# Attention and two feed-forward stages on one core: moving the first h products, the last output tiles and a score wait

## The chip, the cores and the metric

The kernel runs on one core of a Trainium2 chip. The metric is the time of one execution in device microseconds (us). The kernel before takes 922.23 us, the median of three runs from 921.72 to 922.34.

Engines are named as in the profile: PE is TensorE's matmul, PEld its weight load, DVE VectorE, ACT ScalarE, POOL GpSimd, SP SyncE, which issues the DMAs. A name such as SPq is the sequencer of that engine.

## The reference

Batch 4, 8 heads, 576 positions, head dimension 64; then 2304 tokens of width 512.

```python
scores = scale * np.matmul(q, k.transpose(0, 1, 3, 2))
cum = np.cumsum(np.maximum(s, 0.0), axis=-1)
bias = -(cum[:, :, :, None] - cum[:, :, None, :])
scores = np.where(causal, -1000000000.0, scores + np.minimum(bias, 0.0))
attn = softmax(scores)                     # max taken off, sum + 1e-9
x = (attn @ v), heads side by side         # (2304, 512)
x = ((x @ w1) * (x @ w2)) @ w3 @ w_out     # inner width 1024
h = x @ w_in                               # width 2048
out = (h - np.tanh(h)) @ w_out2            # (2304, 512)
```

## The kernel before

All instructions are collected as operations with the buffers they read and write, a priority (a small number goes first), and for some a choice of engines (ACT, DVE or POOL). A list planner (class Plan) plays them through with costs and the numbers in PARAM, picks on each engine the ready operation with the smallest priority, and writes the result out. The order on each engine, and which engine does an operation, is fixed from then on. On the chip an engine works its list in order and waits where data are late. Where the planner expects PE to wait in the first 66 us, it puts dummy matmuls (`filler`, line 576) into the list.

Stages, in order of time:

1. Attention, head by head (`head`), 32 heads. For the eight heads of batch 0 (`full`) a score tile is one matmul in full f32 over 69 rows (line 688; line 686 for the first head): 64 rows of q and k, and five rows of bias. The five bias rows of k are written by two small DMAs (query tiles 0 to 2, and 3 to 4), the five rows of q hold a pattern that picks one of them for each query tile. In the other batches the operands are split into two parts of f32r (`split`: a high part by `copy`, a low part by `sub`, lines 410 to 414) and there are two matmuls (lines 690, 691). Transposes are line 745, the products with v line 772.
2. `products` (line 826): x @ w1 and x @ w2 with split operands, three matmuls for each product. The weights w1, w2 are converted from 64-bit inputs on ACT and DVE first (`convert`, lines 515 to 522). The result goes to DRAM (c_d).
3. w3 @ w_out in one matrix (lines 941 to 943), and operands for stage 5.
4. `x2_block(j)`, j = 0 to 5, 384 tokens each (lines 978 to 980): c @ (w3 @ w_out), two halves n of four groups d of twelve matmuls. Priority 1.2e6 + 100 j + 10 n + d. The results are copied to xs (j = 0, 1) or to xd tiles, which are stored to DRAM (xf_d).
5. Three passes of eight steps (`step`, 24 in all). h = x @ w_in goes by Strassen-like seven products of half size (`product`, line 1055, six matmuls each), with operands x2b (seven tiles) and ws (13 slots, seven used by a step; loaded from ws_d in the order ORDER). Products are accumulated on PSUM banks a, b, c; `taken` copies a bank to a temporary (on ACT mostly), `plus` (line 1064, DVE) adds a bank and a temporary. Each of the four sums of a step goes through `gated` (lines 1078 to 1087: u, sq, th, pg, mk on ACT and DVE, then gh and gl), and then three output tiles of three matmuls each (lines 1095 to 1097, with voh and vol, the split w_out2) are accumulated on banks 0 to 5. After a pass the six banks are copied to osb tiles (two of them) and stored.

SBUF is handed out by pools that open and close in the course of the kernel. `pre` (left) opens before the x2 products and holds seven x2b tiles, ws0 to ws6, and the first NPRE = 12 of 16 w_out2 pairs. `p2` (right) opens when the x2 products have let go of their operands (xp, wap and cp closed) and holds all else of stage 5: the other ws slots, gh, gl, u, sq, th, pg, mk, osb. The seven temporaries (cst0 to 2, asb0 to 3) live from stage 2 to the end.

The parts around the change:

Of the kernel before, what the change touches and what calls it, by code (L numbers as in the profile page):

```python
# [40 lines left out]
PARAM = dict(tail=346719, dsub2=2687.6, dcopy2=-363.2, dother2=15239, act2=-1777.4, pool2=4728.0, cs=1176.5, xs=-29.3, layw=10048, x2p=785.3, nwst=3, late=778.7,  # L41
             gate=4314.0, cst=6240.0, ramp0=1010.9, ramp1=-512.9, dsub=4382.6, dsub0=-2390.3, dcopy=-1480.1, dcopy0=-572.5, dother=1106.1, dother0=-2029.8,
             spi=2833.6, lay=0, layp=641747, layf=473733, dve0=1000.0, early=120052, raw0=0, rawp=-700.0, ng=8, nosb=2, cut=(), convq=2713.8, natb=8, nfull=8,
             wap=1402502, dve=1000.0, act=-598.5, pool=-114.4, sem=160.0, pesem=180.0, slow=1.1, convp=3444.2, npre=12, nbias=3, keep=0.5, ff=0.0, fu=66000,
             wlast=0, kbp=-210.2, qk=2491.2, kb=-1761.7, rv=-1179.0, st=83.8, fl=756.2, iv=1391.7, pv=-1105.8, ml=4388.9, bw=370.0, ntr=3, actb=1, actn=0,
             spp=3043.5, ne=2, nsb=2, ncf=5, outlag=187.2, o_qk=-577.9, o_kb=647.6, o_rv=179.7, o_iv=-2316.9, o_fl=-889.6, o_pv=-374.3, o_ml=-281.5, o_st=829.5,
             o_c0=-132.5, o_c1=211.6, o_c2=404.2, o_c3=3145.8, o_c4=-302.4, o_c5=1092.9, o_c6=-321.1, o_c7=-538.4, o_c8=-309.2, o_c9=568.4, o_c10=-644.8,
             o_c11=721.4, o_c12=620.5, o_c13=-386.2, o_c14=-1078.1, o_c15=-517.3, o_h0=-2746.5, o_h1=-2197.2, o_h2=507.3, o_h3=211.0, o_h4=-153.0, o_h5=1351.8,
             o_h6=-1038.9, o_h7=-501.6, o_h8=-600.0, o_h9=726.1, o_h10=-463.4, o_h11=308.3, o_h12=1634.4, o_h13=837.2, o_h14=-1715.4, o_h15=-171.3, o_h16=-831.4,
             o_h17=198.0, o_h18=-178.6, o_h19=1097.2, o_h20=517.6, o_h21=-1252.5, o_h22=177.5, o_h23=337.0, o_h24=-1368.9, o_h25=-531.3, o_h26=724.9, o_h27=-159.5,  # L50
             o_h28=2096.8, o_h29=-111.9, o_h30=-510.2, o_h31=-973.2)
# [289 lines left out]
def tile_kernel(ctx, tc, qk, v, s, w1, w2, w3t, w_out, w_in, w_out2, out):  # L341
# [108 lines left out]
    cst_r = abp.ring("cst", 3, [P, TB])  # L450
    asb_r = abp.ring("asb", 4, [P, TB])
# [4 lines left out]
    rqk = [att.buf(f"rqk{i}", [P, 2 * S], n=3) for i in range(2)]  # L456
# [29 lines left out]
    xs_r = cp.ring("xs", 10, [P, XB])  # L486
    xd_r = cp.ring("xd", 4, [P, XB])
# [3 lines left out]
    p2 = Pool("p2", "right")  # L491
    x2b = [p_.buf(f"x2b{i}", [P, 2, 2, XB], F32R, n=4) for i, p_ in enumerate([pre] * 7 + [p2])]
# [14 lines left out]
    osb_r = p2.ring("osb", PARAM["nosb"], [P, DM], n=2)  # L507
# [90 lines left out]
    for e in e2[:1] + [None] + e2[1:]:  # L598
        if e is None:
            zero([lambda: ssum.t], [20], [ssum], -5, 1.0)  # L600
            for R in rqk:
                a = 0 if R is rqk[0] else S
                pl.op([("POOL", 1040.0 if a == 0 else 560.0, lambda R=R, a=a: nc.gpsimd.memset(R.t[D:D + 5, a:], 0.0))], w=[(R, (1, 2))], prio=-2300)
        else:
            zero([later(e, EOFF[0], EOFF[0] + D, low)], [D], [(e, 0)], -10 if e is e2[0] else 92, r=scan)
# [32 lines left out]
    def role(n, b):  # L638
        return PARAM[n] + (PARAM["o_" + n] if b == 0 else 0.0)

    def head(h, full, groups=(0, 1)):
# [32 lines left out]
        def softmax_tile(t):  # L674
            q0, q1 = QT[t]
            nq = q1 - q0
            p_ = pr + role("st", b) * t
            bi, bo = msk, (512 if nq < P else S) - q1
            pieces = [(0, q1)] if q1 <= 512 else [(0, HALF), (HALF, S)]
            for n, (k0, k1) in enumerate(pieces):  # L680
                bk = s_ring.next()

                def mm(bk=bk, k0=k0, k1=k1):
                    o_ = bk.t[:nq, :k1 - k0]
                    if one:
                        nc.tensor.matmul(bk.t[:, :k1 - k0], rq()[:D + 5, q0:q0 + P], rk()[:D + 5, k0:k1], start=True, stop=False)
                    elif full:
                        nc.tensor.matmul(bk.t[:, :k1 - k0], rq()[:D + 5, q0:q0 + P], rk()[:D + 5, k0:k1], start=True, stop=True)  # L688
                    else:
                        nc.tensor.matmul(o_, Q.t[:, q0:q1], KH.t[:, k0:k1], start=True, stop=False)  # L690
                        nc.tensor.matmul(o_, Q2.t[:NR, q0:q1], KL.t[:NR, k0:k1], start=False, stop=True)  # L691
                if one:
# [3 lines left out]
                    pe(f_mm4(k1 - k0), mm, [R], [bk], p_ - 2000.0)  # L696
# [261 lines left out]
    x2_ring = Ring(bank[0:8])  # L958
    held = {}

    def x2_block(j):
# [21 lines left out]
        for d in range(KC):  # L983
            x = (xd_r if p else xs_r).next()
            held[l, d] = x
            copy(lambda x=x, d=d: x.t, lambda d=d: bks[d].t[:, :XB], XB, [bks[d]], [x], 1.9e5, psum=True)
            if p:
                dma(lambda d=d: xf_d.t[p, l, d], lambda x=x: x.t, P * XB * 4, [x], [(xf_d, (p * 2 + l) * KC + d)], 2.2e5, row=1536, issue=580.0)
        if j == 1:
            for kg in range(2):  # L990
                operands(kg, [held[y, z * 2 + kg] for z, y in ((0, 0), (0, 1), (1, 0), (1, 1))], xs_r, 2.2e5,
                         lambda i, x, kg=kg: split(lambda: X0[i].t[:, kg, 0], (X0[i], kg * 2), lambda: X0[i].t[:, kg, 1], (X0[i], kg * 2 + 1), lambda: x.t, XB, [x], 2.2e5, kind="xs"))
# [55 lines left out]
    def step(p, fp, pos, X, W):  # L1048
        pr, last = 3.0e5 + pos, p == NPAIR - 1 and fp == NFP - 1

        def product(n, i, bk, first):
# [4 lines left out]
            pe(f_op(6 * f_mm(XB)), mm, [W[i], X[i]], [bk], 2.0e6 + pos + n // 2 * 45 + n % 2)  # L1056
# [64 lines left out]
        if fp == NFP - 1:  # L1121
            for l in range(2):
                for n in range(3):
                    ob, t0, bk = osb_r.next(), p * 2 * XB + l * XB + n * P, bank[l * 3 + n]
                    for a, z in ((0, 256), (256, 512)) if last else ((0, 512),):
                        copy(lambda ob=ob, bk=bk, a=a, z=z: ob.t[:, a:z], lambda bk=bk, a=a, z=z: bk.t[:, a:z], z - a, [bk], [(ob, int(a > 0))] if last else [ob], pr, psum=True)
                    dma(lambda t0=t0: out[t0:t0 + P, :], lambda ob=ob: ob.t, P * DM * 4, [ob], [], 0)

    for p in range(NPAIR):
# [7 lines left out]
        for fp in range(NFP):  # L1137
# [3 lines left out]
            W = {}  # L1141
            for n, i in enumerate(ORDER):
# [49 lines left out]
```

## Time and profile before

| | us |
|---|---|
| median of three runs | 922.23 |
| the profiled execution | 921.88 |
| its span, first to last instruction | 920.2 |
| PE busy | 906.6 (99%) |
| PEld busy | 790.6 (86%) |
| DVE busy | 790.7 (86%) |
| ACT busy | 549.0 (60%) |
| POOL busy | 112.1 (12%) |
| mean granted clock of PE | 0.997 |

Busy is the time in which an engine had an instruction in hand. Matmuls overlap, and their ends are modelled: a matmul of 384 columns is shown as 0.33 us, while the next starts 0.17 us later. The distance of starts tells PE's pace better than the busy time.

### The profile page before, as it was taken

The numbers are of one execution on the slowest core, as the hardware profiler recorded it, in microseconds if no ns is written. First come the engines' busy times: TensorE is split into PE (matmuls) and PEld (weight loads), VectorE is DVE, ScalarE is ACT, GpSimd is POOL, SyncE is SP. The second block draws the span as 40 slices with busy tenths as digits, with TensorE's granted clock in tenths as the row PEclk, the third lists the DMA queues.
The fourth block names the chain that finished last, engine by engine and source line by source line (L and its number), as shares of the span: only waits on it lengthen the run. The fifth ranks groups of instructions, "written<-read, shape, count | busy, mean of one in ns | idle before, by whom it ended". The sixth has DMA issues, their size and how long they took to land.

```text
span 920.2 us, 15850 instructions
## 1 busy us (share of the span) xinstructions
PE 906.6 (99%) x5174; PEld 790.6 (86%) x5174; DVE 790.7 (86%) x1884; ACT 549.0 (60%) x1292; POOL 112.1 (12%) x106
## 2 busy tenths in 40 slices
PE   9999999999999999999999989999999999999996
PEld 7777788888887888988999988989898998989885
DVE  8999999899999599989536999999998878787874
ACT  6998854343423013555446577777787667776765
POOL 1000044545442172000000000000000000000000
PEclk9999999999999999999999999999999999999998
DMA  7677766456565458898877595787977448644401
GB/s 222 202 227 194 217 203 213 130 186 212 177 220 161 154 179 279 275 296 282 270 231 236 189 306 173 255 275 236 387 236 260 116 117 304 200 116 123 115 12 69
DMA packets 102948, 189.94 MB, mean 206 GB/s; under 512 B 10594, under 2 KB 50690, under 8 KB 102867
## 3 DMA queue, kind: packets, MB, share of 16 engines
q1 hardware_dynamic: 102866, 188.94, 64.8%
q8 instruction: 41, 0.67, 0.3%
q14 instruction: 41, 0.33, 0.1%
HBM read 137.20 MB, written 48.01 MB: 201 GB/s over the span
## 4 chain that ended last, share of the span: by engine, by line
PE 89%; DVE 5%; DMA 3%; ACT 1%; issue 1%; SPq 0%; ACTq 0%; DVEq 0%
PE bank L826 21%; PE bank L1055 18%; PE bank L1096 7%; PE bank L1097 7%; PE bank L1095 7%; PE bank L745 5%; PE bank L772 5%; PE bank L979 2%; PE bank L978 2%; PE bank L980 2%; PE bank L690 2%; PE bank L688 2%; PE bank L691 2%; PE bank L941 2%; PE bank L942 2%; PE bank L943 2%
## 5 line engine op out<-in xcount | busy, mean ns | idle before, releaser
L1055 PE MATMUL bank<-x2b,ws 128*128 128x384 f32 x1008 | 192.9, 337 | 2.8 <-DMA ws<-ws_d 1.3
L1055 PEld LDWEIGHTS bank<-x2b,ws 128*128 128x128 f32 x1008 | 178.8, 188 | 12.1 <-DVE asb L1064 3.0
L711 ACT ACTIVATE e<-e,nmx 64x64 f32<-64x64 f32 (+4 forms) x160 | 89.1, 558 | 95.6 <-DVE nmx L705 95.0
L1097 PE MATMUL bank<-voh,gl 128*128 128x512 f32 x288 | 113.8, 395 | 0.0
L1096 PE MATMUL bank<-vol,gh 128*128 128x512 f32 x288 | 113.6, 394 | 0.0
L1095 PE MATMUL bank<-voh,gh 128*128 128x512 f32 x288 | 111.9, 389 | 0.0
L410 ACT ACTIVATE gh<-pg 128x384 fp32r<-128x384 f32 x96 | 50.0, 521 | 46.8 <-DVE pg L1087 46.5
L745 PE MATMUL bank<-ident,e 128*128 128x128 f32 (+1 forms) x480 | 75.4, 275 | 0.8 <-ACT e L711 0.7
L705 DVE CUSTOM_DVE_ANT_0 e<-bank,msk 64x64 f32<-64x64 f32 (+4 forms) x160 | 64.7, 420 | 4.5 <-PE bank L691 3.9
L1064 DVE TENSOR_TENSOR asb<-bank,cst 128x384 f32<-128x384 f32 x72 | 40.0, 555 | 33.2 <-PE bank L1055 32.8
L980 PE MATMUL bank<-xh,wal 128*128 128x384 f32 x192 | 64.1, 334 | 0.0
L978 PE MATMUL bank<-xh,wah 128*128 128x384 f32 x192 | 64.1, 334 | 0.0
L979 PE MATMUL bank<-xl,wah 128*128 128x384 f32 x192 | 64.1, 334 | 0.0
L1097 PEld LDWEIGHTS bank<-voh,gl 128*128 128x128 f32 x288 | 54.0, 187 | 11.5
L826 PE MATMUL bank<-xh,w2h 128*128 128x512 f32 (+1 forms) x160 | 63.3, 396 | 0.0
L745 PEld LDWEIGHTS bank<-ident,e 128*128 128x128 f32 (+1 forms) x480 | 53.8, 131 | 11.0 <-ACT e L711 2.3
L826 PE MATMUL bank<-xh,w1h 128*128 128x512 f32 (+1 forms) x160 | 63.1, 394 | 0.1
L1096 PEld LDWEIGHTS bank<-vol,gh 128*128 128x128 f32 x288 | 54.0, 187 | 9.0
L1095 PEld LDWEIGHTS bank<-voh,gh 128*128 128x128 f32 x288 | 54.1, 188 | 8.6
L515 ACT ACTIVATE wt<-wraw 128x512 f32<-128x512 f32 x62 | 41.4, 671 | 31.0 <-DMA wraw<-w3t 16.7
L826 PE MATMUL bank<-xh,w1l 128*128 128x512 f32 (+1 forms) x160 | 59.4, 371 | 0.0
L1087 DVE COPY_PREDICATED pg<-mk,th 128x384 f32<-128x384 uint32 x96 | 57.8, 602 | 1.9
(144 smaller groups left out, 2190.9 us busy)
## 6 DMA issues: line engine op xcount, KB each, us to landing
ws<-ws_d SPq DMA_DIRECT2D x168, 256.0 KB
ws_d<-wst SPq DMA_DIRECT2D x56, 256.0 KB
rqk<-qk SPq DMA_DIRECT2D x24, 576.0 KB
wraw<-w_out SPq DMA_DIRECT2D x24, 512.0 KB
x_d<-x2s SPq DMA_DIRECT2D x28, 384.0 KB
x2b<-x_d SPq DMA_DIRECT2D x14, 768.0 KB
wraw<-w SPq DMA_DIRECT2D x16, 512.0 KB
wraw<-w_in SPq DMA_DIRECT2D x16, 512.0 KB
```

Source lines behind the costliest of these rows:

```text
L705: nc.vector.tensor_tensor_reduce(e.t[:nq, EOFF[t] + k0:EOFF[t] + k1], bk.t[:nq, :k1 - k0], bi.t[:nq, bo + k0:bo + k1], -0.125, 3.0e38 if f ...
L711: act(lambda: nc.scalar.activation(et(), et(), AF.Exp, bias=nmx.t[:nq, i, tm:tm + 1], scale=-1.0, accum_out=ssum.t[:nq, pj, t, i:i + 1]), ...
L745: nc.tensor.transpose(bk.t[:rows, (at + m) * P:(at + m + 1) * P], e.t[:, EOFF[t] + c * P:EOFF[t] + c * P + rows], ident.t)
L826: nc.tensor.matmul(bk.t[:, :w], w_.t[:, k, f * P:(f + 1) * P], x_.t[:, k, :w], start=k == 0 and i == 0, stop=k == KC - 1 and i == 2)
L978: nc.tensor.matmul(bk.t[:, :XB], wah.t[:, f, a], ch, start=f == 0, stop=False)
L979: nc.tensor.matmul(bk.t[:, :XB], wah.t[:, f, a], cl, start=False, stop=False)
L980: nc.tensor.matmul(bk.t[:, :XB], wal.t[:, f, a], ch, start=False, stop=f == NF - 1)
L1055: nc.tensor.matmul(bk.t[:, :XB], W[i].t[:, kg, a], X[i].t[:, kg, z], start=first and kg == 0 and m == 0, stop=kg == 1 and m == 2, skip_gro ...
L1087: dve(lambda: nc.vector.copy_predicated(pg.t, mk.t.bitcast(U32), th.t), XB, [mk, th], [pg], pr, two=True)
L1095: nc.tensor.matmul(o.t, gh.t[:, a], voh[f].t, start=fp == 0 and f == fp + l * NFP, stop=False)
L1096: nc.tensor.matmul(o.t, gh.t[:, a], vol[f].t, start=False, stop=False)
L1097: nc.tensor.matmul(o.t, gl.t[:, a], voh[f].t, start=False, stop=fp == NFP - 1 and f == fp + (1 - l) * NFP)
```

## The change

1. **h products of step 0.** Their priority falls from 2.0e6 + ... to 1.2e6 + 510.9 - 0.4 n (n the number of the product, 0 to 6), among those of the second half of the last x2 block (1.2e6 + 510 to 513). The x2 ring of banks begins at bank 4, so that the last block uses banks 0 to 3. x2b of the first pass is made with priority 260216 instead of 2.2e5.
2. **Weight slots.** Step 1 takes slots ws0 to ws6 again, step 2 begins at ws7.
3. **Gate tiles.** One u, sq, th, pg, mk and one pair gh, gl move to `pre`, as do the four xd tiles, which serve as the second u, sq, th, pg. NPRE falls from 12 to 10, the xs ring from 10 tiles to 9.
4. **Last output tiles.** The six tiles of the last pass go to the seven temporaries instead of the two osb tiles; the first three are copied whole, the other three in two halves as before.
5. **67-row scores.** Scores of query tiles 0 to 2 use 67 rows and do not wait for the second bias DMA.
6. **PARAM.** The planner's numbers (priorities, engine biases) are others nearly throughout.

```diff
-PARAM = dict(tail=346719, ..., convq=2713.8, ..., convp=3444.2, npre=12, ...
+PARAM = dict(x0=260216, hx=510.9, hxs=-0.4, tail=340436, ..., convq=5942.0, ..., convp=4462.1, npre=10, ...
...
-    rqk = [att.buf(f"rqk{i}", [P, 2 * S], n=3) for i in range(2)]
+    rqk = [att.buf(f"rqk{i}", [P, 2 * S], n=4) for i in range(2)]
...
-    xs_r = cp.ring("xs", 10, [P, XB])
-    xd_r = cp.ring("xd", 4, [P, XB])
+    xs_r = cp.ring("xs", 9, [P, XB])
...
+    xd_r = pre.ring("xd", 4, [P, XB])
...
-    gh_r = p2.ring("gh", PARAM["ng"], [P, XB], F32R)
-    gl_r = p2.ring("gl", PARAM["ng"], [P, XB], F32R)
-    u_r = p2.ring("u", 2, [P, XB])
-    sq_r = p2.ring("sq", 2, [P, XB])
-    th_r = p2.ring("th", 2, [P, XB])
-    pg_r = p2.ring("pg", 2, [P, XB])
-    mk_r = p2.ring("mk", 1, [P, XB])
+    u_r, sq_r, th_r, pg_r, mk_r = (pre.ring(n, 1, [P, XB]) for n in ("u", "sq", "th", "pg", "mk"))
+    gh_r, gl_r = (Ring([(p2 if i else pre).buf(f"{n}{i}", [P, XB], F32R) for i in range(PARAM["ng"])]) for n in ("gh", "gl"))
+    for x, y in zip((u_r, sq_r, th_r, pg_r), xd_r.bufs):
+        x.bufs.append(y)
...
-                    (t1 - t0) * qb * 4, [(rel, range(t0, t1))], [(R, 2)], pr + role("kb", b), issue=760.0)
+                    (t1 - t0) * qb * 4, [(rel, range(t0, t1))], [(R, 3 if t0 else 2)], pr + role("kb", b), issue=760.0)
...
+            kr, have = (D + 3, [(R, (0, 1, 2))]) if t < 3 else (D + 5, [R])
...
-                    pe(f_mm4(k1 - k0), mm, [R], [bk], p_)
+                    pe(f_mm4(k1 - k0), mm, have, [bk], p_)
...
-    x2_ring = Ring(bank[0:8])
+    x2_ring = Ring(bank[4:8] + bank[0:4])
...
-            pe(f_op(6 * f_mm(XB)), mm, [W[i], X[i]], [bk], 2.0e6 + pos + n // 2 * 45 + n % 2)
+            pe(f_op(6 * f_mm(XB)), mm, [W[i], X[i]], [bk], 2.0e6 + pos + n // 2 * 45 + n % 2 if pos else 1.2e6 + PARAM["hx"] + n * PARAM["hxs"])
...
-                    ob, t0, bk = osb_r.next(), p * 2 * XB + l * XB + n * P, bank[l * 3 + n]
-                    for a, z in ((0, 256), (256, 512)) if last else ((0, 512),):
+                    ob, t0, bk = (tmp_r if last else osb_r).next(), p * 2 * XB + l * XB + n * P, bank[l * 3 + n]
+                    for a, z in ((0, 256), (256, 512)) if last and l else ((0, 512),):
...
+            if p == 0 and 0 < fp < 3:
+                w_r.i = (fp - 1) * 7
```

## Rows read from the trace of the kernel before

**Rows 1.** The page, part 1: busy us (share of the span) and instructions

```profile
PE 906.6 (99%) x5174; PEld 790.6 (86%) x5174; DVE 790.7 (86%) x1884; ACT 549.0 (60%) x1292; POOL 112.1 (12%) x106
```

**Rows 2.** Windows of line 576 alone: stretch, us, PE busy, PEld busy, clock, DMA

```profile
0.00:20.00 20.00, 9.52 (x130) 8.88 (x130) 1.00 0.71 200
20.00:66.00 46.00, 2.98 (x36) 2.46 (x36) 1.00 0.74 221
```

**Rows 3.** Windows, all engines: PE, PEld, DVE, ACT, POOL busy, clock, DMA

```profile
532.83:543.84 11.01, 8.25 (x43) 7.05 (x43) 9.82 (x20) 7.41 (x16) 0.00 (x0) 1.00 0.87 272
559.00:574.67 15.67, 15.67 (x80) 14.11 (x79) 15.67 (x35) 12.71 (x28) 0.00 (x0) 1.00 0.51 145
```

**Rows 4.** Timeline of PE, 513 to 545: start, us, instruction, [idle before, releaser]

```profile
512.73 0.33 PE L979 MATMUL bank<-xl,wah 128*128 128x384 f32 x1
...
532.66 0.33 PE L980 MATMUL bank<-xh,wal 128*128 128x384 f32 x1
532.83 2.25 PE L1055 MATMUL bank<-x2b,ws 128*128 128x384 f32 x12
535.44 3.65 PE L1055 MATMUL bank<-x2b,ws 128*128 128x384 f32 x18 [0.36 <-ACT xd L410]
540.21 2.35 PE L1055 MATMUL bank<-x2b,ws 128*128 128x384 f32 x12 [1.12 <-DVE asb L1064]
543.84 1.45 PE L1055 MATMUL bank<-x2b,ws 128*128 128x384 f32 x7 [1.27 <-DMA ws<-ws_d]
```

**Rows 5.** Windows, all engines, the last x2 products

```profile
500.00:532.83 32.83, 32.83 (x191) 32.83 (x190) 32.55 (x67) 21.51 (x44) 0.00 (x0) 1.00 0.61 201
```

**Rows 6.** Timeline of SP, 515 to 545: loads of ws

```profile
538.72 6.20 SPq L407 DMA_DIRECT2D ws<-ws_d  x10
```

**Rows 7.** Groups of DVE instructions, 800 to 900: count, busy us, mean ns

```profile
L1087 DVE COPY_PREDICATED pg<-mk,th 128x384 f32<-128x384 uint32 x25 | 15.0, 601 | 0.7
...
L1064 DVE TENSOR_TENSOR asb<-bank,cst 128x384 f32<-128x384 f32 x20 | 11.1, 555 | 17.1 <-PE bank L1055 17.0
```

**Rows 8.** Timeline of DVE, 470 to 640: the thirteenth vol

```profile
584.71 0.70 DVE L414 TENSOR_TENSOR vol<-wt,voh 128x512 fp32r<-128x512 f32 x1
```

**Rows 9.** Chain of waits, 909 to 921: start, us, what

```profile
910.11 2.03 DMA out<-osb
...
912.24 0.67 ACT osb L410 x2
...
915.79 0.38 ACT osb L410
```

**Rows 10.** Timeline of PE, 911.5 to 913

```profile
911.72 0.39 PE L1097 MATMUL bank<-voh,gl 128*128 128x512 f32 x1
...
912.40 0.39 PE L1097 MATMUL bank<-voh,gl 128*128 128x512 f32 x1
```

**Rows 11.** Windows, one microsecond of the tail; last column GB/s

```profile
911.00:912.00 1.00, 1.00 (x6) 0.81 (x6) 0.00 (x0) 0.00 (x0) 0.00 (x0) 1.00 1.03 379
```

**Rows 12.** Groups of PE by shape: count, busy us, mean ns

```profile
L688 PE MATMUL bank<-rqk 69*128 69x448 f32 x14 | 6.5, 545 | 0.0
...
L695 PE MATMUL bank<-rel,e 96*128 96x448 f32 x2 | 0.9, 538 | 0.0
```

**Rows 13.** Timeline, 0 to 21: before the scores of the second head

```profile
13.17 0.71 SPq L407 DMA_DIRECT2D rqk<-rel  x1
...
14.90 1.95 PE L576 MATMUL bank<-msk 128*128 128x128 bf16 x32
...
17.28 1.33 PE L576 MATMUL bank<-msk 128*128 128x128 bf16 x21
...
18.45 2.06 PE L688 MATMUL bank<-rqk 69*128 69x64 f32 x8
```

**Rows 14.** Windows, all engines, attention of batch 0

```profile
40.00:50.00 10.00, 10.00 (x81) 7.52 (x81) 9.88 (x35) 9.50 (x31) 0.00 (x0) 1.00 0.78 220
```

**Rows 15.** Windows of line 826 alone: PE busy and count, PEld busy

```profile
63.30:100.00 36.70, 15.97 (x57) 9.76 (x57) 1.00 0.73 206
```

More of the change, by code (lines that the diff above doesn't have):

```diff
@@ L40 @@
 NR = D + 10
[L41 to L51, printed above, removed]
@@ new lines @@
+PARAM = dict(x0=260216, hx=510.9, hxs=-0.4, tail=340436, dsub2=1528.8, dcopy2=-853.5, dother2=14612, act2=-1842.4, pool2=3809.8, cs=1084.2, xs=-910.7, layw=11256,
+             x2p=802.9, nwst=3, late=1242.6, gate=3438.6, cst=9989.9, ramp0=938.3, ramp1=-594.7, dsub=4928.8, dsub0=-3223.5, dcopy=-1519.6, dcopy0=-452.2,
+             dother=2155.0, dother0=-2182.1, spi=5413.1, lay=0, layp=807319, layf=632083, dve0=1000.0, early=104995, raw0=0, rawp=-700.0, ng=8, nosb=2, cut=(),
+             convq=5942.0, natb=8, nfull=8, wap=1395833, dve=1000.0, act=-513.6, pool=1168.4, sem=160.0, pesem=180.0, slow=1.1, convp=4462.1, npre=10, nbias=3,
+             keep=0.5, ff=0.0, fu=66000, wlast=0, kbp=-1030.7, qk=3742.8, kb=-2301.5, rv=-661.3, st=52.2, fl=726.8, iv=1782.3, pv=-710.6, ml=4374.4, bw=370.0,
+             ntr=3, actb=1, actn=0, spp=1650.8, ne=2, nsb=2, ncf=5, outlag=189.4, o_qk=-65.6, o_kb=311.0, o_rv=127.7, o_iv=-1759.7, o_fl=-761.0, o_pv=-374.8,
+             o_ml=29.5, o_st=715.5, o_c0=-431.5, o_c1=-221.0, o_c2=415.6, o_c3=3189.4, o_c4=-318.8, o_c5=1024.1, o_c6=-73.0, o_c7=-444.6, o_c8=-150.2, o_c9=710.9,
+             o_c10=-683.9, o_c11=878.3, o_c12=763.7, o_c13=-946.4, o_c14=-1215.8, o_c15=-1485.3, o_h0=-3622.6, o_h1=-2098.2, o_h2=729.7, o_h3=387.1, o_h4=-463.1,
+             o_h5=1659.9, o_h6=-994.3, o_h7=-218.7, o_h8=-1018.4, o_h9=130.5, o_h10=-51.1, o_h11=146.2, o_h12=2648.6, o_h13=550.3, o_h14=-1141.7, o_h15=-260.0,
+             o_h16=-508.3, o_h17=702.8, o_h18=-207.9, o_h19=1105.1, o_h20=949.4, o_h21=131.0, o_h22=235.0, o_h23=538.4, o_h24=-1625.4, o_h25=-484.1, o_h26=610.1,
+             o_h27=-399.0, o_h28=1907.5, o_h29=-740.9, o_h30=-544.6, o_h31=-939.7)
@@ L449, in tile_kernel @@
     abp = Pool("abp", "left")
-    cst_r = abp.ring("cst", 3, [P, TB])
-    asb_r = abp.ring("asb", 4, [P, TB])
+    cst_r = abp.ring("cst", 3, [P, TB], n=2)
+    asb_r = abp.ring("asb", 4, [P, TB], n=2)
     att = Pool("att", "right")
@@ L685, in mm @@
                     if one:
-                        nc.tensor.matmul(bk.t[:, :k1 - k0], rq()[:D + 5, q0:q0 + P], rk()[:D + 5, k0:k1], start=True, stop=False)
+                        nc.tensor.matmul(bk.t[:, :k1 - k0], rq()[:kr, q0:q0 + P], rk()[:kr, k0:k1], start=True, stop=False)
                     elif full:
-                        nc.tensor.matmul(bk.t[:, :k1 - k0], rq()[:D + 5, q0:q0 + P], rk()[:D + 5, k0:k1], start=True, stop=True)
+                        nc.tensor.matmul(bk.t[:, :k1 - k0], rq()[:kr, q0:q0 + P], rk()[:kr, k0:k1], start=True, stop=True)
                     else:
@@ L985, in x2_block @@
             held[l, d] = x
-            copy(lambda x=x, d=d: x.t, lambda d=d: bks[d].t[:, :XB], XB, [bks[d]], [x], 1.9e5, psum=True)
+            copy(lambda x=x: x.t, lambda d=d: bks[d].t[:, :XB], XB, [bks[d]], [x], 1.9e5, psum=True)
             if p:
@@ L1123, in step @@
                 for n in range(3):
-                    ob, t0, bk = osb_r.next(), p * 2 * XB + l * XB + n * P, bank[l * 3 + n]
-                    for a, z in ((0, 256), (256, 512)) if last else ((0, 512),):
-                        copy(lambda ob=ob, bk=bk, a=a, z=z: ob.t[:, a:z], lambda bk=bk, a=a, z=z: bk.t[:, a:z], z - a, [bk], [(ob, int(a > 0))] if last else [ob], pr, psum=True)
+                    ob, t0, bk = (tmp_r if last else osb_r).next(), p * 2 * XB + l * XB + n * P, bank[l * 3 + n]
+                    for a, z in ((0, 256), (256, 512)) if last and l else ((0, 512),):
+                        copy(lambda ob=ob, a=a, z=z: ob.t[:, a:z], lambda bk=bk, a=a, z=z: bk.t[:, a:z], z - a, [bk], [(ob, int(a > 0))] if last and l else [ob], pr, psum=True)
                     dma(lambda t0=t0: out[t0:t0 + P, :], lambda ob=ob: ob.t, P * DM * 4, [ob], [], 0)
```

10 lines of the change are left out of this document (5 added, 5 removed).

## The prediction

> **What bounds the kernel now.** I read the shares of the page first. TensorE is busy 906.6 us of a span of 920.2 [rows 1], so there is no large stretch in which another engine sets the time: what a change can win is the time in which TensorE does nothing useful, and that has to be found stretch by stretch. Three places are left.
>
> The first is the start. The kernel issues dummy matmuls of line 576 where the planner expects TensorE to wait; they count as busy. They fill 9.52 us of the first 20 us and 2.98 us of the 46 us after that [rows 2]; from 66 us on there are none.
>
> The second is the passage from the x2 products (lines 978 to 980) to the first gating step (line 1055). Between 532.83 and 543.84 us TensorE is busy 8.25 of 11.01 us; in a whole later step, which repeats every 15.67 us, it is never idle [rows 3]. The timeline shows the gaps: 0.36, 1.12 and 1.27 us, ended by the copy xd, by a DVE sum, and by the load of the next step's weights [rows 4]. The reader should go by starts, though: from 512.73 to 532.83 there are 116 starts of x2 matmuls, one in 0.1733 us, and at that pace the 12 + 18 + 12 = 42 matmuls up to 543.84, of the same 384 columns, need 7.28 us. 11.01 - 7.28 = 3.73 us are lost, not the 2.76 that "busy" leaves, because a matmul with no successor behind it still shows its whole 0.33 us. The 42 matmuls are exactly the seven h products of step 0, six each.
>
> The Trainium skill ("Perfetto Trace Analysis", Identifying the Most-Contended Engine) says that the busy share of the matmuls is no measure of how near TensorE is to its limit, since pipelined matmuls mislead. The trace agrees: by busy time this place is worth 2.76 us, by starts 3.73.
>
> The third is the tail. The last matmul starts at 912.40 and is over at 912.79 [rows 10]; the span ends 7.4 us later. In the chain of waits the last 10 us are output copies and two waits for a store, the first of 2.03 us: there are two osb tiles for six output tiles, so the third and the fifth tile's copies wait until a store has released theirs [rows 9].
>
> **The change, part by part.** *h products of step 0 among the last x2 products.* Their priority becomes 1.2e6 + 510.9 - 0.4 n, which is that of the second half of the last x2 block (1.2e6 + 510 to 513). Their banks 5 to 7 are free by then, as the x2 ring now begins at bank 4 and the last block takes banks 0 to 3; their operands x2b and weights ws0 to 6 lie in the early pool already. Four groups of 12 x2 matmuls (4 x 2.08 us) are there to put between the products, and each product that waits for a copy or a sum (0.555 us for a sum [rows 7], plus handover) has such a group, or another product, to cover it. At best the 3.73 us go. Left over can be what is late next, and there are two candidates.
>
> (a) Step 1's weights. Now ten loads are queued on SP from 538.72 on, for 6.20 us [rows 6], because seven slots are in use and the six others belong to the pool that opens only when the x2 products are over. After: step 1 takes slots 0 to 6 again, each free once its step-0 product has read it, so the first loads can be issued about 8 us sooner. I count this wait (1.27) as gone. The SP queue carries these loads past w_out loads and x2 stores that wait in it; a stop there would bring it back.
>
> (b) The gates (4 to a step). The first tile's u, sq, th, pg, mk lie in the early pool; the second of each (but mk) is one of the four xd tiles, which the last x2 block writes and stores. pg of gate 2 is xd3. The x2 products now end at 532.83 + 7.28 = 540.1; copy to some 540.8; store some 2.0 us (as in [rows 9]) to 542.9; then five gate operations of 0.55 to 0.6 us [rows 7], with handovers about 3.2 us: gate 2's output matmuls can start at about 546. Behind them in the order stand gates 3 and 4, which share mk. TensorE has for 540.1 to 546: two products of step 1 (2.08), the nine matmuls of gate 1 (9 x 0.227 = 2.04), and three more products (3.1) that hang on one another's copies. 7.2 us of work for 6 us, but with waits in it: I take 0.5 us lost, bounds 0 and 3.73 (that the gap merely comes later). So this part gives 3.2 us.
>
> What hides the DVE work: step 0 has five sums and four gates of five operations, about 5 x 0.555 + 4 x 2.8 = 14 us, which now start about 8 us sooner, while DVE is busy 32.55 of 32.83 us [rows 5]: nothing is free. What gives way are conversions of w_out2 (vol). The thirteenth is made only at 584.71 [rows 8]; a step uses two, so the first two of those that wait are those of step 6, six steps of 15.67 us after 543.84. The cover is ample; if the order put gate work before the splits of the last x2 block instead, TensorE would wait for those up to these 14 us. Two conversions (npre 12 to 10) go behind the opening of the second pool, ten DVE operations of at most 0.70 us [rows 8], wanted at step 5: nothing. One xs tile less, and x2b made at a later priority while its products come some 8 us sooner: if one is late, its product goes back towards its old place, which the 3.73 us bound; nothing.
>
> *Last output tiles from idle temporaries.* The six tiles are written into the seven temporaries, which are read by sums and gates alone, and those precede the last output matmuls. No copy waits for a store. The banks come free at TensorE's pace, three matmuls in 0.68 us (911.72 to 912.40 [rows 10], 0.227 each); ACT takes 0.67 for two halves [rows 9], so it just follows. The last bank is ready at 912.79, the last copy at about 913.4 (913.2 if DVE takes a half), where now it is 916.18 (915.79 + 0.38 [rows 9]): 2.8 us. A store moves 0.26 MB, 0.69 us at the 379 GB/s of [rows 11], as fast as tiles come, so the queue holds at most one tile. From the last copy to the end the span has 4.0 us now, and I leave that. Bounds: 2.1 (one tile queued more) to 3.0.
>
> *67-row scores.* Matmul time doesn't follow the rows: 448 columns take 545 ns with 69 rows and 538 with 96 [rows 12]. What changes is the wait: scores of the first three query tiles no longer wait for the second small load (rows 3 to 4 of the bias), issued on SP as late as 13.17 for head 1, whose scores start at 18.45 after 32 + 21 dummy matmuls (1.95 and 1.33 us) [rows 13]. At most those 3.3 us can turn into useful work there. DVE is nearly full in this stage (9.88 us of the ten from 40 us on [rows 14]), so part of it comes back later.
>
> *The new numbers of the planner* move everything in the first 100 us: weight conversions rank later (convp 3444 to 4462, convq 2714 to 5942), heads and copies are dealt out anew. The trace can't show the new order. Above, a gain is bounded by all dummy matmuls (12.5 us [rows 2]); below, by the products done before 100 us: 57 matmuls, about 57 x 0.227 = 12.9 us [rows 15], if all had to wait for later weights. Nearest to the 67-row edit are the 3.3 us of fillers; with both I take 1.0 us of gain.
>
> **Sum.** -3.2 - 2.8 - 1.0 = -7.0 us: span 920.2 to 913.2. The profiled execution took 921.88, 1.7 more than its span, so 914.9; the median of the runs is 922.23, 0.35 above that one, so 915.2 us.
>
> **Rivals.** *The gap only moves* (17%). The products still wait on copies, sums and SP-issued loads, or gate 2 holds everything behind the xd stores: 3.73 us lost all the same. For it: each gap in [rows 4] has another releaser, so one cure may uncover the next. Against: four x2 groups of 2.08 us are cover that the products lack now. Only tail and start remain: 922.2 - 3.8 = 918.4.
>
> *The start gives more* (14%). A better order takes 5 us of the 12.5 us of dummies: 922.2 - 3.2 - 2.8 - 5 = 911.2. Against it: the full DVE [rows 14].
>
> *No change* (8%). The new order loses in the first 100 us some 6 us, what the two other places give: 920.4 to 924.1, about 922.
>
> *Slower* (9%): the weights of the first products come too late. Place: 63 to 110 us, where w1 and w2 are converted on a full DVE and TensorE has no dummies to count. Price: up to the 12.9 us of [rows 15]. For it: conversions are what the new numbers move most. Against: attention work can fill in. It decides once the loss exceeds 6.0 + 1.8 = 7.8 us; in full, 922.2 - 6.0 + 12.9 = 929.1.
>
> **Chances.** The forecast has 52%, by itself 912.5 to 918. A measurement of this kernel tells 0.2%, 1.84 us, from no change: faster means under 920.4. Faster 0.52 + 0.17 + 0.14 = 0.83, same 0.08, slower 0.09. The range 909.5 to 920.6 takes in the forecast, the moved gap and most of the better start, and leaves out 2 in 10.
>
> **What would show it.** After: matmuls of line 1055 between those of lines 978 to 980, step 0's seven products over within 1 us of the last x2 matmul, loads of ws issued before it; no wait of ACT for out stores, and a span that ends about 7.4 - 2.8 = 4.6 us after the last matmul. Steps still 15.67 us apart. Fewer than 166 dummy matmuls would show the start's part; about as many, that it gave nothing. The prediction is wrong if TensorE has a gap of over 2 us in the two steps after x2, if a wait for xd stores shows up before gate 2, or if TensorE idles between 60 and 110 us by more than 3 us.

## The result, and the profile after

The changed kernel takes 912.66 us (median of four executions, 912.38 to 913.92); the kernel before, beside it, 922.15 (921.72 to 922.34). The ratio is 0.990, interval 0.9883 to 0.9918: faster by 9.5 us, where 7.0 were forecast (915.2, range 909.5 to 920.6).

The profiled execution took 913.92 with a span of 912.2; the other three had spans of 910.6 to 910.9. Against the 920.2 of before its 8.0 us split at three marks that every trace has, the starts of the first x2 matmul, of the 43rd h matmul and of the last matmul:

| | before | after | difference | forecast |
|---|---|---|---|---|
| span's start to the first x2 matmul | 432.96 | 431.05 | -1.91 | -1.0 |
| from there to the 43rd h matmul (products of step 0 done) | 110.88 | 107.15 | -3.73 | -3.2 |
| from there to the last matmul | 368.56 | 369.51 | +0.95 | 0 |
| from there to the span's end | 7.77 | 4.50 | -3.27 | -2.8 |

(The forecast counted its 7.4 us of tail from the end of the last matmul, 912.79 [rows 10], the table from its start.) In three further traces of the same order of work the two middle rows together are 476.62 to 476.64 us, after 476.66: behind the first x2 matmul the changed kernel repeats itself. The kernel before does so less well: in a second trace with its order of work up to the tail (e2_tail_alone) the second row is 110.18, not 110.88, so that the gap of the prediction cost 3.03 us there and 3.73 here. The first x2 matmul came at 429.8 to 432.8 us (mean 431.1) in nine traces whose order up to it is that of the changed kernel, and at 432.96 and 433.06 in the two of the kernel before. So the 1.5 us that the median gained beyond this trace I put down to scatter of the start; the other three executions left no trace to show it.

Part 1 of the page, to set beside [rows 1]:

```profile
PE 904.5 (99%) x5124; PEld 789.6 (87%) x5124; DVE 797.0 (87%) x1897; ACT 538.9 (59%) x1274; POOL 114.6 (13%) x108
```

Fifty TensorE instructions fewer: all dummies. Windows of the dummies' line, now 573, against [rows 2] (stretch, its length, PE busy, PEld busy, clock, DMA share, GB/s):

```profile
0.00:20.00 20.00, 7.26 (x80) 6.70 (x80) 1.00 0.74 207
20.00:66.00 46.00, 2.83 (x36) 2.44 (x36) 1.00 0.76 224
```

The first 20 us hold 2.26 us less of them, the rest as much as before.

The waits of TensorE (released line: total us, times, longest), the whole list:

```profile
PE bank L688 <- DVE nmx L703: 1.2, 2, 0.6
PE bank L573 <- DVE msk L569: 1.1, 1, 1.1
PE bank L743 <- ACT e L709: 0.5, 1, 0.5
PE bank L743 <- DVE en L411: 0.3, 1, 0.3
```

Nothing in it is on line 1053, the h products (1055 before): the three gaps of [rows 4] have no successor. The timeline of TensorE there (start, us, instruction):

```profile
522.42 0.33 PE L978 MATMUL bank<-xh,wal 128*128 128x384 f32 x1
522.59 1.20 PE L1053 MATMUL bank<-x2b,ws 128*128 128x384 f32 x6
523.63 0.33 PE L976 MATMUL bank<-xh,wah 128*128 128x384 f32 x1
...
525.71 2.24 PE L1053 MATMUL bank<-x2b,ws 128*128 128x384 f32 x12
...
538.02 0.33 PE L978 MATMUL bank<-xh,wal 128*128 128x384 f32 x1
538.19 2.24 PE L1053 MATMUL bank<-x2b,ws 128*128 128x384 f32 x12
540.27 0.39 PE L1093 MATMUL bank<-voh,gh 128*128 128x512 f32 x1
```

Read the starts: from 522.59 to 540.27 stand 54 h and 48 x2 matmuls, 17.68 / 102 = 0.1733 us each, the pace of x2 alone. The Trainium skill's "Perfetto Trace Analysis" (Identifying the Most-Contended Engine) says that the busy share of the matmuls misleads, since they are pipelined. These two traces agree: by busy time 2.76 us could go here, by starts 3.73, and 3.73 went. The groups up to the one at 534.03 are step 0's seven products, over before the last x2 matmul; the group behind it, at 538.19, is already step 1's. Its weights come early; SP's timeline, against the ten loads of [rows 6] that began at 538.72:

```profile
523.82 0.32 SPq L407 DMA_DIRECT2D ws<-ws_d  x1
...
535.38 4.10 SPq L407 DMA_DIRECT2D ws<-ws_d  x5
```

The tail: the last matmul, ACT's last copies after and before, and windows of one microsecond (PE, PEld, DVE, ACT, POOL busy, clock, DMA share, GB/s):

```profile
907.70 0.39 PE L1095 MATMUL bank<-voh,gl 128*128 128x512 f32 x1
```

```profile
906.77 2.02 ACT L410 ACTIVATE asb<-bank 128x256 f32<-128x256 f32 x6
```

```profile
915.06 1.40 ACT L410 ACTIVATE osb<-bank 128x256 f32<-128x256 f32 x4 [1.46 <-DMA out<-osb]
```

```profile
907.00:908.00 1.00, 1.00 (x5) 0.56 (x3) 0.00 (x0) 0.98 (x4) 0.00 (x0) 1.00 1.01 375
908.00:909.00 1.00, 0.09 (x1) 0.00 (x0) 0.00 (x0) 0.76 (x3) 0.00 (x0) 1.00 1.02 373
909.00:910.00 1.00, 0.00 (x0) 0.00 (x0) 0.00 (x0) 0.00 (x0) 0.00 (x0) 1.00 1.03 379
```

The last copy ends 0.70 us behind the last matmul's end (908.79 against 908.09), where it took 3.67 (916.46 against 912.79 [rows 10]). The chain of waits in [rows 9] stops at the first half of the last tile, 915.79 + 0.38 = 916.17; the second half ends 0.3 later. From the last copy to the end are 3.4 us instead of 3.7. The stores now run without a pause at 373 to 379 GB/s until about 910.4. At that rate one takes 0.69 us, and TensorE gives a tile in 0.68 [rows 10]: by this estimate the DMA engines' pace is close behind the copies and would be the next limit.

The start, against [rows 13] (start, us, instruction):

```profile
7.86 1.47 SPq L407 DMA_DIRECT2D rqk<-rel  x2
...
13.65 0.33 PE L686 MATMUL bank<-rqk 67*128 67x64 f32 x2
...
14.59 0.55 PE L573 MATMUL bank<-msk 128*128 128x128 bf16 x7
```

Head 1's scores begin at 13.65 instead of 18.45. Both small loads of its bias rows are issued together at 7.86. Before they were apart (SP's timeline):

```profile
8.77 0.77 SPq L407 DMA_DIRECT2D rqk<-rel  x1
...
15.24 1.28 SPq L407 DMA_DIRECT2D rqk<-rel  x2
```

The second load of head 1 is in the pair at 15.24. The row at 13.17 [rows 13], which the prediction took for it, is the first load of head 2: in the trace's record it carries three bias rows, like the one at 8.77, and the two at 15.24 carry two rows each.

### The profile page after: what moved, and what is told of

Same layout as the page of the kernel before. It is cut to its first block, busy times and chain, and to the rows that moved or that the text cites. A ratio compares the mean times of both kernels' runs of the same rounds, so it can differ in the third digit from the quotient of the medians.

```text
span 912.2 us, 15747 instructions
## 1 busy us (share of the span) xinstructions
PE 904.5 (99%) x5124; PEld 789.6 (87%) x5124; DVE 797.0 (87%) x1897; ACT 538.9 (59%) x1274; POOL 114.6 (13%) x108
## 4 chain that ended last, share of the span: by engine, by line
PE 92%; DVE 6%; DMA 1%; ACT 1%; issue 0%; SPq 0%; ACTq 0%; DVEq 0%
PE bank L1053 19%; PE bank L824 19%; PE bank L1094 7%; PE bank L1095 7%; PE bank L1093 7%; PE bank L743 5%; PE bank L770 4%; PE bank L978 4%; PE bank L976 4%; PE bank L977 4%; PE bank L686 2%; PE bank L688 2%; PE bank L940 2%; PE bank L939 2%; PE bank L941 2%; PE bank L689 1%
## 5 line engine op out<-in xcount | busy, mean ns | idle before, releaser
L1053 PE MATMUL bank<-x2b,ws 128*128 128x384 f32 x1008 | 196.1, 337 | 0.0
L709 ACT ACTIVATE e<-e,nmx 128x576 f32<-128x576 f32 (+4 forms) x160 | 89.1, 558 | 100.7 <-DVE nmx L703 100.2
L410 ACT ACTIVATE wst<-wf 128x256 fp32r<-128x256 f32 x54 | 21.7, 412 | 76.7 <-PE bank L824 35.5
L512 ACT ACTIVATE wt<-wraw 128x512 f32<-128x512 f32 x57 | 38.1, 670 | 36.8 <-DMA wraw<-w3t 16.5
L824 PE MATMUL bank<-xh,w2l 128*128 128x512 f32 (+1 forms) x160 | 59.3, 370 | 0.0
```

The source lines that it names most:

```text
L709: act(lambda: nc.scalar.activation(et(), et(), AF.Exp, bias=nmx.t[:nq, i, tm:tm + 1], scale=-1.0, accum_out=ssum.t[:nq, pj, t, i:i + 1]), ...
L824: nc.tensor.matmul(bk.t[:, :w], w_.t[:, k, f * P:(f + 1) * P], x_.t[:, k, :w], start=k == 0 and i == 0, stop=k == KC - 1 and i == 2)
L1053: nc.tensor.matmul(bk.t[:, :XB], W[i].t[:, kg, a], X[i].t[:, kg, z], start=first and kg == 0 and m == 0, stop=kg == 1 and m == 2, skip_gro ...
```

## The experiments

All ran beside the kernel before, five rounds each; ratios are to it, with their intervals. "Behind" is the time from the first x2 matmul to the last one of the program: 479.44 before, 476.66 after.

**The same kernel again**, no edit.

> The changed kernel once more, unchanged. Its profiled execution (913.92 us) was the slowest of four, the others took 912.4 to 912.7, and its steps stood 15.72 us apart where before they stood 15.68. Theory: that execution was a stray one; the new median is near 912.6, and in a profile near 912.6 the span from the 43rd to the last h and output matmul is again about 368.6 us (369.5 in the stray one). Rival: the new order of matmuls inside a step costs 0.04 us in each of 24 steps, about 0.9 us in every execution; then the same stretch takes 369.5 us again, and the missing 1.3 us are elsewhere.

Ratio 0.9914 (0.9901 to 0.9926); behind 476.64. This is the yardstick for the changed kernel: a difference of 0.3 us behind is readable in a trace, one of 1 us in the medians is not. For the order of before, 0.7 us between its two traces is the measure.

**The tail alone**: the kernel before with this edit.

```diff
-    cst_r = abp.ring("cst", 3, [P, TB])
+    cst_r = abp.ring("cst", 3, [P, TB], n=2)
...
-                    ob, t0, bk = osb_r.next(), p * 2 * XB + l * XB + n * P, bank[l * 3 + n]
-                    for a, z in ((0, 256), (256, 512)) if last else ((0, 512),):
+                    ob, t0, bk = (tmp_r if last else osb_r).next(), p * 2 * XB + l * XB + n * P, bank[l * 3 + n]
+                    for a, z in ((0, 256), (256, 512)) if last and l else ((0, 512),):
```

> The kernel before with only the last six output tiles in the temporaries; every other instruction keeps its place. Theory: the two waits for a store go, and the end moves from 7.4 us behind the last matmul to 4.1 to 4.6: a gain of 2.8 to 3.3 us, so 918.9 to 919.4. Rival: the stores themselves, 1.57 MB at some 380 GB/s, set the end; then the copies are early but the gain is under 2 us, above 920.2.

Ratio 0.9970 (0.9961 to 0.9980), 3.0 us by the medians beside each other; the tail takes 4.81 instead of 7.77, behind 478.74. The 0.7 less is not the edit's: TensorE does the same work in the same order there, and the wait of 0.36 us for xd [rows 4] happens not to occur. The last copy ends 0.69 us behind the last matmul, 2.97 sooner, and the end follows in 3.7 us as before. So the tail's gain stands alone and adds up. The 0.3 by which the changed kernel's tail is shorter still lies behind the landing of the last store (1.36 us to the end, 1.67 in this run and before); that stretch takes 1.0 to 1.7 us over all traces, with either tail.

**69 rows**: the changed kernel, all scores with 69 rows and waiting for every part of their tile.

```diff
-            kr, have = (D + 3, [(R, (0, 1, 2))]) if t < 3 else (D + 5, [R])
+            kr, have = D + 5, [R]
```

> The changed kernel with 69 rows and the wait for both small loads in all scores; the planner writes the same order on every engine, so only the wait differs. Theory of the prediction: waiting for the second load makes scores of the first heads late, up to 1.0 us more: 913.0 to 913.7, with TensorE idle or late before scores of heads 1 to 7. Rival: in the new order the second load is issued right behind the first and has landed long before the scores; nothing changes, 912.7 within 0.3, and the early scores of head 1 (13.65 instead of 18.45 us) come from the planner's new numbers alone.

Ratio 0.9917 (0.9904 to 0.993), the same as after; every engine issues the same order of work. Its start:

```profile
7.69 1.47 SPq L407 DMA_DIRECT2D rqk<-rel  x2
...
14.03 0.33 PE L686 MATMUL bank<-rqk 69*128 69x64 f32 x2
```

The loads are as early as after, and head 1's scores only 0.4 us later. So the 67 rows give nothing, and the early load does not come from them. What is left of that edit is the fourth part of rqk. Before, both small loads of a head wrote "part 2" of the tile, so the planner made the second wait for the first to land (write after write): issued at 8.77, landed at 13.5. The second then stood in SP's list behind three loads of head 2 and went out at 15.24. Now the second writes part 3, and they go out together; the run with the split load alone (below) has the early start too.

**h late**: the changed kernel, step 0's products back at their old priority and step 1's weights in later slots.

```diff
-            pe(f_op(6 * f_mm(XB)), mm, [W[i], X[i]], [bk], 2.0e6 + pos + n // 2 * 45 + n % 2 if pos else 1.2e6 + PARAM["hx"] + n * PARAM["hxs"])
+            pe(f_op(6 * f_mm(XB)), mm, [W[i], X[i]], [bk], 2.0e6 + pos + n // 2 * 45 + n % 2)
...
-            if p == 0 and 0 < fp < 3:
-                w_r.i = (fp - 1) * 7
```

> The changed kernel with the h products of step 0 at their old priority and the weight slots handed out as before; gate tiles, tail, numbers and 67 rows stay. Theory: the gap behind the x2 products comes back, 3.7 us lost by starts before the second step, against some 0.9 us at most lost later now: 2.8 to 3.7 us slower, 915.4 to 916.4. Rival: the new numbers and the early gate tiles had closed the gap already; under 1 us slower, below 913.7.

Ratio 0.9944 (0.9932 to 0.9957); behind 478.28, 1.64 more than in the repeat. To the 43rd h matmul it takes 108.21: of the 3.73 us only 1.06 come back. (In this trace the granted clock is 0.91 between 60 and 80 us, 1.00 there in the repeat, and the first x2 matmul comes only at 432.82; so I read behind it and not by the medians.) TensorE's timeline, then SP's:

```profile
532.69 5.37 PE L1053 MATMUL bank<-x2b,ws 128*128 128x384 f32 x30
538.83 6.77 PE L1053 MATMUL bank<-x2b,ws 128*128 128x384 f32 x36 [0.78 <-DVE asb L1062]
```

```profile
532.71 1.27 SPq L407 DMA_DIRECT2D ws<-ws_d  x3
```

One gap here, for a sum; none for weights or xd. The six later slots belong to the second pool, and step 1's weights go there at 532.71, right behind the last x2 matmul, not 6 us later as in [rows 6]: as I read it, because the xd tiles moved to the early pool, so that the second pool no longer waits for their stores. In the kernel before the last of these stores landed at 538.01, and the load of w_out that stands ahead of the weights in SP's list waited for DVE until 538.31; which of the two held the weights was not separated. The remaining 0.6 us of the 1.64 do not lie in longer steps (15.720 us here and in the repeat): 0.5 of them go at one place near the end of the first pass, at 659.50, where a product waits for a sum and the next start comes 0.56 us later instead of 0.17.

**The old numbers**: the changed kernel with the planner's numbers of before (npre 10, hx and hxs as after; x0, the priority of the first pass's x2b, goes back to its old 2.2e5 too, so that two of the new numbers for the h products stay and not three).

> The changed code with the planner's numbers of before (npre stays 10, the three new numbers for the h products stay). Theory: the new numbers bring the start (the first x2 matmul at 431 instead of 433 us) and cost 0.04 us in each step, while the code closes the passage: first x2 matmul at 433, 107.2 us from it to the 43rd h matmul, steps 15.68 us apart again, the tail of 4.5 us; 922 - 3.7 - 3.3 = 915, about 7 us under the kernel before and 1 over the changed kernel. Rival: the passage needs the new numbers too; then over 108.2 us there, 916 or more.

Ratio 0.9932 (0.992 to 0.9945); start 431.25, behind 478.30 (107.91 to the 43rd h matmul). The structure without the new numbers gives 6.4 us by the medians, where the repeat gave 8.0; the new numbers are worth some 1.7 behind the x2 start and ahead of it nothing that its scatter would show.

**One number back**: the changed kernel with the lag of the gates' output matmuls as before.

```diff
-             ntr=3, actb=1, actn=0, spp=1650.8, ne=2, nsb=2, ncf=5, outlag=189.4, ...
+             ntr=3, actb=1, actn=0, spp=1650.8, ne=2, nsb=2, ncf=5, outlag=187.2, ...
```

> The changed kernel with one number set back: outlag 187.2 instead of 189.4, so that the second output tile of a step's last gate goes ahead of the first two products of the step after the next, as before. The order up to the third step is untouched. Theory: the steps alternate four times between h and output matmuls again instead of six times and stand 15.68 us apart, not 15.72: 0.8 to 0.9 us off the stretch behind the 43rd h matmul (369.5 to 368.6), and 912.7 where the changed kernel takes 913.6. Rival: the longer steps come from busier queues or another place of the tiles, not from the alternation; then 15.72 stays and nothing is won.

Ratio 0.9913 (0.9899 to 0.9927), 912.63 us; behind 476.02, 0.62 less than in the repeat, steps of 15.673 us instead of 15.720 (medians). It gives back two thirds of the +0.95. The h matmuls of one step in the changed kernel:

```profile
608.87 2.27 PE L1053 MATMUL bank<-x2b,ws 128*128 128x384 f32 x12
613.74 1.23 PE L1053 MATMUL bank<-x2b,ws 128*128 128x384 f32 x6
615.50 1.22 PE L1053 MATMUL bank<-x2b,ws 128*128 128x384 f32 x6
617.26 1.22 PE L1053 MATMUL bank<-x2b,ws 128*128 128x384 f32 x6
620.41 2.27 PE L1053 MATMUL bank<-x2b,ws 128*128 128x384 f32 x12
```

and with the old lag:

```profile
612.42 1.23 PE L1053 MATMUL bank<-x2b,ws 128*128 128x384 f32 x6
614.87 2.25 PE L1053 MATMUL bank<-x2b,ws 128*128 128x384 f32 x12
619.04 2.27 PE L1053 MATMUL bank<-x2b,ws 128*128 128x384 f32 x12
623.22 2.27 PE L1053 MATMUL bank<-x2b,ws 128*128 128x384 f32 x12
```

A step has 42 h and 36 output matmuls in both. The longer lag (189.4) puts the first two products of the step after next in between the last gate's two output tiles, so h comes in five groups instead of four. By starts, the group of 12 at 614.87 takes 2.084 us until the next output matmul and the two groups of 6 that stand for it (615.50 and 617.26) 1.062 each, 0.040 more; six output matmuls in one go take 1.389, twice three 2 x 0.698, 0.007 more. All other groups are equal (12 in 2.105 us, for one). Together 0.047 per step. Eighteen steps show it, 0.85 us; with the old lag 0.23 is lost again where the first pass ends, and 0.62 is left.

**Slots late**: the changed kernel without the two lines that send steps 1 and 2 back to slots 0 to 6.

> The changed kernel with the weight slots of steps 1 and 2 handed out as before (step 1 takes ws7 to ws12, which open only behind the x2 products). Theory of the prediction: step 1's loads are issued only then, and the wait of 1.27 us for ws comes back, or more: 1.3 to 3 us behind the 43rd h matmul on top of 369.5. Rival: output matmuls of step 0 are there by then and cover the loads; under 0.3 us.

Ratio 0.9921 (0.9909 to 0.9934); behind 478.07, 1.43 more than in the repeat. The first of its two new waits is the one that was foreseen:

```profile
PE bank L1053 <- DMA ws<-ws_d: 0.6, 1, 0.6
...
PE bank L1053 <- DVE cst L1062: 0.3, 1, 0.3
```

By starts the first costs 0.9 us and the second, 4 us later, 0.6. With h early and the slots late the step-1 products are ready before their weights; h late and slots late together (above) cost hardly more, 1.64. So the h move without the slots is worth 0.2 us; the slots without the move were not tried.

**Own second tiles**: the changed kernel, th and pg with second buffers of their own in the second pool; only u and sq still share with xd.

> The changed kernel with own second th and pg tiles in the late pool instead of xd2 and xd3, so that the second gate does not wait until the stores of xd2 and xd3 have landed. The prediction charged 0.5 us (0 to 3.7) to that hold. Theory after the traces: TensorE is not late there, since h and output matmuls of the first gate cover it: no change in the two stretches (107.15 and 369.5 us), within 0.3. Rival: the hold delays the second to fourth gate and so the steps behind it: 0.5 us or more off 369.5.

Ratio 0.9912 (0.9898 to 0.9925); behind 476.54. Nothing that costs time was held by the stores of xd2 and xd3.

**The split load alone**: the kernel before with rqk in four parts and the second load writing part 3; rows and numbers as before.

```diff
-    rqk = [att.buf(f"rqk{i}", [P, 2 * S], n=3) for i in range(2)]
+    rqk = [att.buf(f"rqk{i}", [P, 2 * S], n=4) for i in range(2)]
...
-                    (t1 - t0) * qb * 4, [(rel, range(t0, t1))], [(R, 2)], pr + role("kb", b), issue=760.0)
+                    (t1 - t0) * qb * 4, [(rel, range(t0, t1))], [(R, 3 if t0 else 2)], pr + role("kb", b), issue=760.0)
```

> The kernel before with one edit: the five bias rows of k count as two parts, one for each of the two small loads, so that the second load no longer waits until the first has landed (both wrote one part). Scores keep 69 rows and wait for both loads. Theory: this wait between two loads, not the rows of a score, kept the scores of head 1 at 18.45 us; both loads now go out back to back near 8 us, head 1's scores start near 14, about 104 instead of 170 dummy matmuls are in the list, and the first x2 matmul comes at 431 instead of 433: 919.5 to 920.5. Rival: the early start is given back later since DVE is full; first x2 matmul at 433 and 922.

Ratio 1.0074 (1.006 to 1.0088): slower. The start gains what it does in the changed kernel (first x2 matmul at 430.19, 100 dummies of line 576 instead of 166), but behind it takes 488.49, 9.05 more than before. The longest waits of TensorE, and two windows:

```profile
PE bank L1055 <- DVE vol L414: 3.5, 1, 3.5
PE bank L1055 <- ACT xd L410: 2.1, 1, 2.1
PE bank L979 <- DVE xl L414: 1.5, 1, 1.5
```

```profile
520.00:540.00 20.00, 17.85 (x93) 17.03 (x92) 18.25 (x36) 11.51 (x23) 0.00 (x0) 0.91 0.64 215
540.00:560.00 20.00, 15.66 (x75) 14.39 (x74) 19.44 (x41) 15.82 (x34) 0.00 (x0) 0.91 0.95 334
```

A faster start changed the order of everything that the planner deals out later, and in the old passage this order meets a conversion (vol) that is not done. The granted clock averages 0.91 of the 2.4 GHz level in both windows, with TensorE idle for 2.1 and 4.3 of the 20 us. The clock has its own share of the 9.05: from 535 to 540 us, right behind the 2.1 us of waiting for xd, it is 0.66, and TensorE, busy for 4.96 us, starts 20 matmuls where 29 would start at 0.1733. Over the two windows I estimate 0.09 x 40 = 3.6 us.

**The numbers alone**: the kernel before with all new numbers (npre 12 kept; x0, hx and hxs are not read by its code).

> The code of before with the planner's new numbers alone (npre 12). Theory: the second load still waits for the first, so head 1 is late as before and the first x2 matmul stays at 432.5 to 433.5; the steps alternate six times and cost 0.04 us more each; the gap of the passage stays, 110 to 111 us from the first x2 to the 43rd h matmul. Together 922 to 923, no gain. Rival: the numbers alone give part of the start or of the passage: 920 or less.

Ratio 1.0121 (1.0104 to 1.0138): slower still, and this is the place that the slower rival named. Windows (PE, PEld, DVE, ACT, POOL busy, clock, DMA share, GB/s):

```profile
60.00:80.00 20.00, 16.72 (x124) 13.64 (x123) 18.54 (x54) 14.94 (x44) 0.00 (x0) 0.93 0.88 239
80.00:100.00 20.00, 18.73 (x130) 14.12 (x130) 19.81 (x63) 17.66 (x50) 0.00 (x0) 0.98 0.56 175
```

TensorE has 18.50 and 19.80 us busy there in the kernel before, 18.19 and 20.00 after. The 48th matmul of the first products starts at 108.53 (95.67 before, 91.79 after); the first x2 matmul comes at 438.35, 5.4 late, and 4.2 more are lost behind it. Whether late weights are the cause isn't shown: TensorE's longest waits between 60 and 112 us are for a load of q (1.8 us) and for e (1.8), none for weights. The last part of w2 is converted at 164.4 instead of 111.8, but in the changed kernel too it comes at 141.3, and the products are not late there.

**The same kernel once more, beside the next one**, no edit.

> The changed kernel, as the one beside which the next is to be read on the same chip. Both theories: 912.5 to 913.7, first x2 matmul within 429.5 to 432, 476.65 us from it to the last matmul.

Ratio 0.9906 (0.9893 to 0.992), 912.97 us; behind 476.64.

**A version meant to beat it**: the changed kernel with the old lag (187.2), and the last output tile copied half by DVE, half by ACT.

```diff
+                        if last and l and n == 2:
+                            if a:
+                                pl.op([("ACT", c_act(z - a, True), lambda ob=ob, a=a, z=z, bk=bk: nc.scalar.activation(ob.t[:, a:z], bk.t[:, a:z], AF.Copy))], r=[bk], w=[(ob, 1)], prio=pr)
+                            else:
+                                pl.op([("DVE", c_dve(z - a), lambda ob=ob, a=a, z=z, bk=bk: nc.vector.tensor_copy(ob.t[:, a:z], bk.t[:, a:z]))], r=[bk], w=[(ob, 0)], prio=pr)
+                            continue
```

> The changed kernel with outlag 187.2 (four alternations in a step) and the last output tile copied half by DVE and half by ACT. Theory: 0.6 us from the steps (476.0 us from the first x2 to the last matmul) and at most 0.3 us from the tail, where the stores at 380 GB/s may take that back: 0.6 to 0.9 us under the changed kernel beside it. Rival: the scatter of the start (2 us) hides it, medians within 0.3.

Ratio 0.9907 (0.9893 to 0.992), 912.84 us: no better than the changed kernel. Behind it has the 0.6 us of the lag (476.04), but the tail takes 4.69. Its timeline:

```profile
908.13 0.38 ACT L1126 ACTIVATE asb<-bank 128x256 f32<-128x256 f32 x1
908.55 0.42 DVE L1128 COPY asb<-bank 128x256 f32<-128x256 f32 x1 [5.60 <-ACT asb L1126]
```

The halves ran one after the other: the last copy ends 0.88 us behind the last matmul, not 0.70, and the tail is longer by as much. The Trainium skill's "PSUM — Partial Sum Buffer" (PSUM bank collisions raise a hardware error) says that two engines may not read one bank in the same partitions at once and that the compiler's scheduler keeps them apart. The trace agrees so far: the DVE half is released by ACT's and starts 0.04 us after it has ended. The planner of this kernel has the same rule in its code, and no run lets both read at once. No version tried here beats the changed kernel by more than the start scatters.

## Why the prediction was right, and where its steps were not

**The passage.** The sum said 3.2 gained; 3.73 went in this pair of traces (3.03 against the second trace of the old order), and 0.95 came back later, 2.8 net. The place, the price by starts and the bound were right. Three steps behind them were not. *Who closes the gap*: I gave all of it to the h products' move, with four x2 groups as cover. With h and slots back in their old places 2.67 of the 3.73 are still gone (e4_h_late), or 2.0 of the 3.03. The wait for weights (1.27 of it) went, as I read it, with the second pool, whose loads start 6 us sooner; how the rest divides between the early tiles and the new numbers stays open. The move and the slots together give the last 1.06, and 0.5 at the end of the first pass. *Step (b), gate 2 held by the xd stores*, for which I took 0.5 us, costs nothing: th and pg tiles of its own change nothing (e8_own_second). The first output matmuls start at 540.27 with TensorE never idle. *What is left over* is instead in the repeated steps, by the planner's lag, a number that I had passed over with the others; "steps still 15.67 us apart" failed by 0.05.

Step (a), the slots, was right: without them the wait for ws is back (0.9 us by starts), and 1.43 us in all (e7_late_slots).

That the net 2.8 is so near to the 3.2 is luck in part: the 0.5 that I took for the gates did not come, and the 0.95 that did was not in the sum.

**The tail.** 2.8 forecast, 3.27 in the traces, of which e2_tail_alone gives 2.96 by itself. The mis-sized term is the point from which it counted: 916.18 is the end of the first half of the last tile, and the last copy ended at 916.46. So it is 3.7 us, not 4.0, from the last copy to the end, and these stay in e2_tail_alone. The copy's 0.6 us behind the last matmul are 0.70. The other 0.3 of the 3.27 lies behind the last store, where the traces scatter. The three windows of 1 us bear out the rate of [rows 11].

**The start.** 1.0 forecast, 1.9 in the trace and up to 1.5 more in the median. The right place (head 1's scores, held by its second small load), the wrong row and the wrong reason. The row at 13.17 is head 2's; the load that I meant came at 15.24. Scores with 67 rows that needn't wait for it do nothing (e3_69_rows). It waited for the first load only because both were declared as writes to the same part of a tile, and then for its turn on SP. I read a late load with a late need and did not ask what held it.

**The rivals.** *The gap only moves* fell: no wait of line 1053 is left. *The start gives more* was the nearest miss: its 911.2 is 1.5 us from the 912.66, my 915.2 is 2.5, the surplus being the start's and the tail's. *Slower* did not happen, but its place is real. The numbers alone do lose there (e10_numbers_alone, 1.2% slower), with products late at 60 to 110 us and a price of 9.2 us of span in the trace, 11.6 by the medians, against my 12.9 at most; late weights as the cause were not shown. What I lacked is that the parts do not add: the numbers lose 9.2 us on the old structure and gain some 1.7 on the new one, and the split load loses 6.2 alone. The new structure takes such shifts upstream with little harm: behind, it needs 476.66 us with the new numbers and 478.30 with the old (e5_old_numbers), the old structure 479.44, 488.49 with the split load and 483.59 with the new numbers.

## What to carry to other kernels

Price a gap between matmuls by the spacing of their starts, and before deciding which edit closes it, list what each wait is released by: here 2.67 of 3.73 us went without the work that was moved into the gap, a good part, as I read it, because a pool could open sooner. Trace the kernel before twice, for the gap itself was 3.0 us in one execution and 3.7 in another. When a load is late, look for its twin, and tell the two apart by their sizes: in this planner two transfers into disjoint rows of one tile wait for each other if the tile has no parts to tell them apart. A chain of waits can end ahead of the last copy; look at the engine's own timeline too. Where a planner deals out the whole order, an edit is worth what it is in the company of the others: the same numbers lost 1.2% on one structure and gained 0.2% on the other.

## What the runs showed of the hardware

Alternating between two kinds of matmul streams cost something though TensorE never idled: in the repeated steps one further group of 384-column matmuls among the 512-column ones took 0.04 us (12 in 2.084 us, twice 6 in 2.124), 0.047 with its counterpart. What in the engine takes it was not looked into.

Six stores of 0.26 MB, issued some 0.7 us apart, ran at 373 to 379 GB/s from 907 to 910 us; with the last copy 0.70 us behind TensorE, these windows leave a faster one little to win. That was not shown, since the halved copy was slower.

The granted clock fell where TensorE stood waiting: in the run with the split load alone it was 1.00 up to 535 us, 0.66 for the 5 us behind a wait of 2.1 us, and 0.79 from 550 to 555, when TensorE was busy again behind a wait of 3.5.
